# Fused attention and two mixtures of experts: lower parts, one-hots and token numbers moved from VectorE to GpSimd, and another order of VectorE's work

## The chip, the cores and the metric

The kernel runs on one core of a Trainium2 chip. The metric is the device time of one execution in microseconds, the median of several runs. Five engines work side by side, each through its own queue in order: TensorE (PE in the profile; its weight loads are PEld), VectorE (DVE), ScalarE (ACT), GpSimd (POOL) and SyncE (SP). Here SyncE issues the DMAs of the weights and GpSimd the indirect ones, which gather and scatter rows by token number.

## The reference, cut to what matters

Causal attention over 4 batches, 12 heads, 448 positions and 64 channels gives a matrix x of 1792 tokens by 768 channels. Two mixtures of experts follow, each with 8 experts of 768 x 1024 and 1024 x 768.

```
# layer one: only tokens with x @ w_skip > 0 go to an expert
e = argmax(x @ w_gate);  gate = softmax(x @ w_gate)[e]
x = x + gate * (relu(x @ w1[e]) @ w2[e])
# layer two: every token, by the cosine to the experts' embeddings
e = argmax((x/|x|) @ (emb/|emb|).T / tau);  gate = softmax(...)[e]
out = gate * (relu(x @ w1[e]) @ w2[e])
```

## The kernel before, in words

The attention stage comes first and ends at about 230 us. It leaves x in memory, the router's choice for layer one and, for both layers, a table of token numbers by expert in tiles of 128. The expert layers follow: layer one from about 240 to 520 us, a short turn, layer two from 530 us to the end.

**Split numbers.** The products are made in a reduced float32 format. Every operand is therefore split into an upper part (a rounding copy, ScalarE) and a lower part (operand minus upper part, VectorE), and a product takes three terms: upper by upper, lower by upper, upper by lower. For the weights these are split_high (L736) and split_low (L740), on chunks of 128 rows: six chunks of w1, 1024 wide, and eight of w2, 768 wide, per expert. The lower part is written over the raw weights. For the tokens the split is in xt_split (L760, L761), for the activations in split_ht: ScalarE's relu gives the upper part (L772), VectorE the lower one (L773), which reads the transposed h from PSUM and the upper part from SBUF.

**A visit.** One tile of 128 tokens through one expert is a Tile object with two halves, begin and finish. begin has both halves of layer 1 (layer1, L781), the copy of h (copy_h, L940), its transposes (turn_h, L798), its split, and layer 2 over chunks 0 to 5 (layer2, L789). finish has chunks 6 and 7, between them the transposes of the next visit's tokens (L754), and put_y, which scales the result into py. The first visit of an expert also splits its w2 (w2_high, w2_low) between the matmuls, and at the end of begin the first two chunks of the next expert's w1 (ahead, L966 to L970). The last finish of an expert splits chunks 2 to 5 of that w1 and orders the loads of weights further on (L212, L218).

**Branches.** Behind the first begin of an expert stands a branch on the number of further visits (L1107), inside it others (L1088). Where an expert has one visit, every engine steps over the body; an operation behind the branch on a buffer that the body also uses (the three transpose tiles tp among them) waits until the engine it depends on has come out of it. For the input measured here the visits are, by expert 0 to 7: layer one 1, 1, 1, 1, 2, 1, 1, 4; layer two 1, 2, 3, 4, 1, 2, 4, 1; together 30. An expert with two visits uses for its second the tokens of g_r, gathered inside the branch (L1109 in layer two, before finish is written) by a DMA from GpSimd's queue.

**Layer one's router for layer two.** In layer one each visit also finds the expert of layer two for the tokens of the visit before: route_enter (L878: two one-hots multiplied into the table of token numbers), route_turn, route_logits, route_pick with the scatter of py (L856), route_rank, and in finish route_put, which makes row and column (list_place) and from them the one-hots roh and voh (L176, L178). put_y then notes the token numbers: pidx (L812), and in layer one pinv and pv (L814, L815).

**Layer two's norm.** gate_parts gives six steps per visit: the sum of squares (ScalarE, L907), a first guess (L139, L140), three rounds of three small VectorE operations (L143 to L145), and the gate: three operations (L148 to L150), an exponential on ScalarE (L911) and two more (L912, L913). self.step() issues the next of them at the place where it is written, so that its place in begin is its place in the queues. In layer one the list is empty.

The order of everything in this part is written out by hand (manual_schedule): the order of the calls in begin and finish is the order in each engine's queue.

Of the kernel before, what the change touches and what calls it, by code (L numbers as in the profile page):

```python
# [13 lines left out]
ALU = mybir.AluOpType  # L14
# [10 lines left out]
NTOK = B * S  # L25
P = 128
# [4 lines left out]
NONE = 2048  # L31
ROW1 = DM + 1
ROW2 = DM + NE
BIG = float(1 << 20)
# [11 lines left out]
def moe_attention_kernel(tc, qk, vv, w_r, emb, tau, w11, w12, w21, w22, out):  # L46
    nc = tc.nc
# [24 lines left out]
    with ExitStack() as top:  # L72
# [98 lines left out]
        def one_hots(eng, n, row, col, v, roh, voh, which=(0, 1), between=lambda: None):  # L171

            for j in which:
                between()
                if j == 0:
                    eng.tensor_scalar(roh, count[:n], row, None, op0=ALU.is_equal)  # L176
                else:
                    eng.tensor_scalar(voh, count[:n, 0:NCOL], col, v, op0=ALU.is_equal, op1=ALU.mult)  # L178
# [506 lines left out]
        with ExitStack() as ctx:  # L685
# [20 lines left out]
            pidx = keep([P, 1], I32, "pidx")  # L706
# [31 lines left out]
            def split_low(i, c, eng):  # L738
                hi, lo, raw = chunk(i, c)
                eng.tensor_tensor(lo, raw, hi.bitcast(F32), op=ALU.subtract)  # L740
# [61 lines left out]
            def put_y(m, g, idx):  # L802
                for u in range(2):
                    s_ = slice(u * (DM // 2), (u + 1) * (DM // 2))
                    if m == 0:
                        nc.vector.scalar_tensor_tensor(
                            py[:, s_], p2[u], g[:, DM : DM + 1], g[:, s_], op0=ALU.mult, op1=ALU.add)
                    elif u == 0:
                        nc.scalar.activation(py[:, s_], p2[u], AF.Copy, scale=gate2)
                    else:  # L810
                        nc.vector.tensor_scalar(py[:, s_], p2[u], gate2, None, op0=ALU.mult)  # L811
                nc.vector.tensor_copy(pidx, idx)  # L812
                if m == 0:
                    nc.vector.tensor_scalar(pinv, idx, float(NTOK - 1), BIG, op0=ALU.is_gt, op1=ALU.mult)  # L814
                    nc.vector.tensor_scalar(pv, idx, -float(NONE), None, op0=ALU.add)  # L815

            def put_out():
                nc.gpsimd.indirect_dma_start(  # L818
# [23 lines left out]
            def route_pick():  # L842
                mx = rooms["mx2"]
                nc.vector.tensor_reduce(out=mx, in_=pm[:, 0:8], axis=AX.X, op=ALU.max)
                d = py[:, DM:]
                nc.vector.tensor_scalar(d, pm[:, 0:8], mx, None, op0=ALU.subtract)
                eq = rooms["eq2"]
                nc.vector.scalar_tensor_tensor(eq, d, 0.0, wtie[:, 0:8], op0=ALU.is_equal, op1=ALU.mult)
                bm = rooms["bm2"]
                nc.vector.tensor_reduce(out=bm, in_=eq, axis=AX.X, op=ALU.max)  # L850
                nc.vector.tensor_tensor(bm, bm, pinv, op=ALU.max)
                oh = rooms["oh2"]
                nc.vector.tensor_scalar(oh, eq, bm, None, op0=ALU.is_equal)
                nc.vector.tensor_scalar(bm, bm, -float(CT), float(NE * CT), op0=ALU.mult, op1=ALU.add)
                rt.update(base=bm, oh=oh, eq=eq)
                nc.gpsimd.indirect_dma_start(  # L856
                    out=x2, out_offset=bass.IndirectOffsetOnAxis(ap=pidx, axis=0),
                    in_=py, in_offset=None, bounds_check=NTOK - 1, oob_is_err=False)
# [5 lines left out]
            def route_put(fills=None):  # L864
                if fills is None:
                    nc.vector.tensor_tensor(run[:, 1, :], run[:, 1, :], rt["oh"], op=ALU.add)
                rk = rooms["rk2"]
                nc.vector.tensor_tensor_reduce(
                    out=rt["eq"], in0=pm[:, 8:16], in1=rt["oh"], scale=1.0, scalar=0.0,
                    op0=ALU.mult, op1=ALU.add, accum_out=rk)  # L870
                fill = lambda: fills.pop(0)() if fills else None
                row, col = list_place(None, P, rk, rt["base"], None, fill, rooms["lp"])
                roh = rooms["roh2"]
                voh = rooms["voh2"]
                one_hots(nc.vector, P, row, col, pv, roh, voh, between=fill)

            def route_enter(last=False):
                nc.tensor.matmul(pm[:, 16 : 16 + NCOL], rooms["roh2"], rooms["voh2"], start=True, stop=True)  # L878
# [63 lines left out]
            class Tile:  # L942
# [23 lines left out]
                def ahead(self, k):  # L966

                    if self.first and self.i + 1 < len(experts):
                        split_high(self.i + 1, k)
                        split_low(self.i + 1, k, nc.vector)  # L970

                def begin(self):
                    i, route = self.i, self.m == 0 and self.prev
                    if self.m == 1 and self.prev:
                        put_out()
                    self.step()
                    self.w2_high(0, 1, 2, 3)
                    layer1(i, 0, range(4), False)
                    layer1(i, 1, range(3), False)
                    layer1(i, 0, range(4, KC), False)  # L980
                    self.step()
                    layer1(i, 0, range(KC), True)
                    if route:

                        route_enter()
                    self.w2_low(0, 1)
                    copy_h(0)
                    self.w2_high(4)
                    self.step()
                    self.w2_low(2, 3)  # L990
                    self.step()
                    layer1(i, 1, range(3, KC), False)
                    if i == 0 and not self.prev:
                        late_hots()
                        enter_late()
                    if route:
                        route_turn()
                    state["tp"] = 2
                    turned = turn_h(0)
                    self.step()  # L1000
                    split_ht(turned, 0)
                    while self.norm:
                        self.step()
                    layer1(i, 1, range(KC), True)
                    copy_h(1)
                    self.w2_high(5, 6, 7)
                    if route:
                        route_logits()
                    self.w2_low(4)
                    if route:  # L1010
                        route_pick()
                    self.w2_low(5)
                    layer2(i, 0)
                    layer2(i, 1)
                    turned = turn_h(1)
                    split_ht(turned, 4)
                    self.w2_low(6, 7)
                    layer2(i, 2)
                    layer2(i, 3)
                    if route:  # L1020
                        route_rank()
                    self.ahead(0)
                    self.ahead(1)
                    layer2(i, 4)
                    layer2(i, 5)
# [181 lines left out]
```

## Time and profile before

| | us |
|---|---|
| median of 3 runs | 903.12 (901.76 to 904.38) |
| the profiled execution's own time | 902.78 |
| span from its first to its last instruction | 901.1 |
| TensorE busy | 824.0 |
| VectorE busy | 554.4 |
| ScalarE busy | 474.8 |
| GpSimd busy | 135.2 |

The profile is of one execution. In a timeline row stand the start in us from the span's start, the duration, the engine, the line of the kernel and the operation, what is written and read, how many instructions of the kind were merged (xN), and in brackets the engine's idle time before it with what ended it. "DVEq" is VectorE's queue (a branch, a semaphore). A wait for several semaphores is put down to the one that came last, and now and then to the instruction that stands behind the true one.

### The profile page before, as it was taken

How to read it: one execution, taken by the hardware profiler on the slowest of the kernel's cores; microseconds unless marked ns; L12 is line 12 of the kernel's file. 1: busy time of each engine (PE TensorE's matmuls, PEld its weight loads, DVE VectorE, ACT ScalarE, POOL GpSimd, SP SyncE). 2: the span in 40 equal slices, each digit the busy share in tenths (PEclk: the TensorE clock that was granted, in tenths of full speed). 3: DMA queues.
4: the chain of work that ended last, by engine and by line, in shares of the span. 5: the costliest groups of instructions: out<-in, count | busy, mean ns of one | idle time of the engine just before them, and what ended most of it. 6: DMA issues, size and time to landing. Idle time of an engine off the chain costs nothing. (4 is left out here: it accounts for less than half of the span.)

```text
span 901.1 us, 14898 instructions
## 1 busy us (share of the span) xinstructions
PE 824.0 (91%) x4960; PEld 686.5 (76%) x4960; DVE 554.4 (62%) x1641; ACT 474.8 (53%) x1013; POOL 135.2 (15%) x150
## 2 busy tenths in 40 slices
PE   7998989989797899899999879899999998999994
PEld 5665766666487788788899748789889887889884
DVE  5767767776566688378833476665283268574343
ACT  5777666666455466166612336454272256463252
POOL 1132404013201111011010021011111011110100
PEclk9999999999899899999999999999999999999998
DMA  8979565563636487267710354580451086361000
GB/s 243 315 271 299 165 185 165 167 206 139 202 140 258 175 300 286 72 232 300 299 45 28 145 198 159 197 332 21 149 211 51 19 313 267 133 238 41 37 1 18
DMA packets 59032, 158.22 MB, mean 176 GB/s; under 512 B 13013, under 2 KB 23765, under 8 KB 58448
## 3 DMA queue, kind: packets, MB, share of 16 engines
q1 hardware_dynamic: 52816, 139.33, 43.4%
q0 software_dynamic: 6080, 17.29, 5.4%
q8 instruction: 59, 0.97, 0.5%
q14 instruction: 77, 0.63, 0.2%
HBM read 146.45 MB, written 22.92 MB: 188 GB/s over the span
## 5 line engine op out<-in xcount | busy, mean ns | idle before, releaser
L789 PE MATMUL p<-hi,ht 128*128 128x384 f32 x960 | 241.8, 353 | 8.5 <-DVE ht L773 4.6
L740 DVE TENSOR_TENSOR lo<-raw,hi 128x768 fp32r<-128x768 f32 (+1 forms) x218 | 220.6, 1062 | 8.0 <-ACT hi L736 4.5
L781 PE MATMUL p<-hi,xt 128*128 128x512 f32 x720 | 183.3, 403 | 8.0 <-PEq L1088 3.3
L736 ACT CAST hi<-raw 128x768 fp32r<-128x768 f32 (+1 forms) x218 | 187.3, 923 | 0.6 <-DMA raw<-in_w 0.6
L789 PEld LDWEIGHTS p<-hi,ht 128*128 128x128 f32 x960 | 167.8, 191 | 14.7 <-DVE ht L773 10.6
L781 PEld LDWEIGHTS p<-hi,xt 128*128 128x128 f32 x720 | 140.4, 198 | 37.4 <-ACTq L1088 5.1
L321 ACT ACTIVATE pr<-st,mn 112x336 f32<-112x336 f32 x192 | 99.5, 520 | 60.4 <-DVE mn L318 60.4
L789 PE MATMUL p<-lo,ht 128*128 128x384 f32 x480 | 124.3, 340 | 0.4 <-issue 0.4
L773 DVE SCALAR_TENSOR_TENSOR ht<-tp,ht 128x512 fp32r<-128x512 f32 x60 | 41.4, 689 | 115.3 <-ACT ht L772 106.6
L781 PE MATMUL p<-lo,xt 128*128 128x512 f32 x360 | 96.2, 402 | 0.0
L940 ACT COPY hs<-p 128x512 f32<-128x512 f32 x60 | 34.8, 580 | 106.0 <-PE p L781 67.0
L789 PEld LDWEIGHTS p<-lo,ht 128*128 128x128 f32 x480 | 88.7, 191 | 0.5 <-issue 0.5
L760 ACT CAST xt<-tp 128x384 fp32r<-128x384 f32 (+2 forms) x62 | 30.4, 492 | 109.5 <-PE tp L754 108.8
L761 DVE TENSOR_TENSOR xt<-tp,xt 128x384 fp32r<-128x384 f32 (+2 forms) x62 | 33.3, 544 | 84.5 <-ACT xt L760 81.6
L318 DVE CUSTOM_DVE_ANT_0 st<-s,mask 112x336 f32<-112x336 f32 x144 | 63.5, 465 | 29.4 <-PE s L307 17.8
L781 PEld LDWEIGHTS p<-lo,xt 128*128 128x128 f32 x360 | 67.8, 195 | 11.4
L772 ACT ACTIVATE ht<-tp 128x512 fp32r<-128x512 f32 x60 | 36.0, 600 | 55.1 <-PE tp L798 49.4
L331 PE MATMUL tp<-ident,pr 112*112 112x112 f32 x480 | 57.3, 267 | 0.0
L307 PE MATMUL s<-qk 64*112 64x112 f32 (+2 forms) x288 | 49.6, 450 | 7.1 <-DVE mn L318 7.1
L331 PEld LDWEIGHTS tp<-ident,pr 112*112 112x112 f32 x480 | 47.1, 136 | 8.6 <-issue 7.8
L818 POOL DMA_INDIRECT out<-py,pidx x18 | 19.7, 1093 | 207.7 <-ACT hi L736 75.5
L342 PE MATMUL av<-pt,v 112*64 112x448 f32 (+3 forms) x384 | 50.6, 405 | 0.0
(201 smaller groups left out, 908.3 us busy)
## 6 DMA issues: line engine op xcount, KB each, us to landing
raw<-in_w SPq DMA_DIRECT2D x96, 512.0 KB
raw<-in_w SPq DMA_DIRECT2D x128, 384.0 KB
qk<-in_qk SPq DMA_DIRECT2D x23, 896.0 KB
x<-x SPq DMA_DIRECT2D x24, 448.0 KB
v<-in_vv SPq DMA_DIRECT2D x4, 1344.0 KB
qk<-in_qk SPq DMA_DIRECT2D x2, 448.0 KB
g_n<-x,L POOLq DMA_INDIRECT x23, 4.4
out<-py,pidx POOLq DMA_INDIRECT x18, 3.4
```

The costliest lines, as they stand in the source:

```text
L307: nc.tensor.matmul(a[c], src[r : r + 64, c * CP : (c + 1) * CP], src[r : r + 64, S : S + n], start=True, stop=True)
L318: nc.vector.tensor_tensor_reduce(out=so, in0=a[c], in1=mask[:, S - n : S], scale=-0.125, scalar=3.0e38, op0=ALU.add, op1=ALU.min, accum_ou ...
L321: return lambda: nc.scalar.activation(a["pr"][:, OFF[c] * CP : OFF[c] * CP + n], so, AF.Exp, bias=mn, scale=-1.0, accum_out=rs)
L331: nc.tensor.transpose(tp[:, u * CP : (u + 1) * CP], pr[:, o : o + CP], ident[:CP, :CP])
L342: nc.tensor.matmul(av[u * D : (u + 1) * D, j * CP :], v_t[b][:, j, 2 * hp + u, :], pts[2 * g + u][:, o : o + (NCH - j) * CP], start=(j == ...
L736: copy(hi, raw)
L740: eng.tensor_tensor(lo, raw, hi.bitcast(F32), op=ALU.subtract)
L772: nc.scalar.activation(hi, src, AF.Relu)
L773: nc.vector.scalar_tensor_tensor(lo, src, 0.0, hi.bitcast(F32), op0=ALU.max, op1=ALU.subtract)
L781: nc.tensor.matmul(p1[u], xt[:, k, :, j], r[:, u * 512 : (u + 1) * 512], start=(k == 0 and j == 0 and not low), stop=(k == KC - 1 and low))
L789: mm = nc.tensor.matmul(p2[u], l, r[:, u * (DM // 2) : (u + 1) * (DM // 2)], start=(f == 0 and j == 0), stop=(f == FC - 1 and j == len(ter ...
L940: nc.scalar.copy(hs[:, u * 512 : (u + 1) * 512], p1[u])
```

## The change

- ahead: the lower parts of the first two chunks of the next w1 go from VectorE to GpSimd.
- route_put: the one-hots go to GpSimd, but for the call at the turn that has other work to put between (fills).
- put_y: pidx, pinv and pv go to GpSimd.
- begin: the lower part of the first half of h (split_ht) now stands in front of chunks 2 and 3 of w2; of the norm, the first round goes behind chunk 4 of w2, the second between chunks 6 and 7, the third and the gate behind chunk 7.

```
--- before.py
+++ after.py
@@ -809,10 +809,10 @@
                         nc.scalar.activation(py[:, s_], p2[u], AF.Copy, scale=gate2)
                     else:
                         nc.vector.tensor_scalar(py[:, s_], p2[u], gate2, None, op0=ALU.mult)
-                nc.vector.tensor_copy(pidx, idx)
+                nc.gpsimd.tensor_copy(pidx, idx)
                 if m == 0:
-                    nc.vector.tensor_scalar(pinv, idx, float(NTOK - 1), BIG, op0=ALU.is_gt, op1=ALU.mult)
-                    nc.vector.tensor_scalar(pv, idx, -float(NONE), None, op0=ALU.add)
+                    nc.gpsimd.tensor_scalar(pinv, idx, float(NTOK - 1), BIG, op0=ALU.is_gt, op1=ALU.mult)
+                    nc.gpsimd.tensor_scalar(pv, idx, -float(NONE), None, op0=ALU.add)
 
             def put_out():
                 nc.gpsimd.indirect_dma_start(
@@ -872,7 +872,7 @@
                 row, col = list_place(None, P, rk, rt["base"], None, fill, rooms["lp"])
                 roh = rooms["roh2"]
                 voh = rooms["voh2"]
-                one_hots(nc.vector, P, row, col, pv, roh, voh, between=fill)
+                one_hots(nc.vector if fills is not None else nc.gpsimd, P, row, col, pv, roh, voh, between=fill)
 
             def route_enter(last=False):
                 nc.tensor.matmul(pm[:, 16 : 16 + NCOL], rooms["roh2"], rooms["voh2"], start=True, stop=True)
@@ -967,7 +967,7 @@
 
                     if self.first and self.i + 1 < len(experts):
                         split_high(self.i + 1, k)
-                        split_low(self.i + 1, k, nc.vector)
+                        split_low(self.i + 1, k, nc.gpsimd)
 
                 def begin(self):
                     i, route = self.i, self.m == 0 and self.prev
@@ -986,9 +986,6 @@
                     self.w2_low(0, 1)
                     copy_h(0)
                     self.w2_high(4)
-                    self.step()
-                    self.w2_low(2, 3)
-                    self.step()
                     layer1(i, 1, range(3, KC), False)
                     if i == 0 and not self.prev:
                         late_hots()
@@ -997,10 +994,8 @@
                         route_turn()
                     state["tp"] = 2
                     turned = turn_h(0)
-                    self.step()
                     split_ht(turned, 0)
-                    while self.norm:
-                        self.step()
+                    self.w2_low(2, 3)
                     layer1(i, 1, range(KC), True)
                     copy_h(1)
                     self.w2_high(5, 6, 7)
@@ -1009,12 +1004,17 @@
                     self.w2_low(4)
                     if route:
                         route_pick()
+                    self.step()
                     self.w2_low(5)
                     layer2(i, 0)
                     layer2(i, 1)
                     turned = turn_h(1)
                     split_ht(turned, 4)
-                    self.w2_low(6, 7)
+                    self.w2_low(6)
+                    self.step()
+                    self.w2_low(7)
+                    while self.norm:
+                        self.step()
                     layer2(i, 2)
                     layer2(i, 3)
                     if route:
```

## Rows read from the trace of the kernel before

**Rows 1.** The page's first part: busy time and share of the span by engine.

```profile
PE 824.0 (91%) x4960; PEld 686.5 (76%) x4960; DVE 554.4 (62%) x1641; ACT 474.8 (53%) x1013; POOL 135.2 (15%) x150
```

**Rows 2.** Waits of TensorE from 240 to 901 us: total, times, longest.

```profile
PE tp L754 <- DVEq L1107: 9.5, 6, 2.7
...
PE p L789 <- DVE ht L773: 4.6, 4, 1.7
...
PE p L789 <- DVE tn_a L148: 3.8, 3, 1.3
...
PE p L781 <- DVEq L1088: 2.5, 2, 1.5
...
PE pm L878 <- DVE voh L178: 1.4, 6, 0.5
```

**Rows 3.** Timeline of VectorE, expert 5 of layer one: start, us, instruction.

```profile
404.15 4.09 DVE L740 TENSOR_TENSOR lo<-raw,hi 128x768 fp32r<-128x768 f32 x4
...
416.57 0.25 DVE L176 TENSOR_SCALAR roh<-count,lq_r 128x128 f16<-128x128 bf16 x1
...
416.74 0.30 DVE L178 TENSOR_SCALAR voh<-count,lq_o,pv 128x112 f16<-128x112 bf16 x1
```

**Rows 4.** Timeline of TensorE: the first transposes behind four branches; idle time in brackets.

```profile
287.26 0.52 PE L754 MATMUL tp<-ident,g_r 128*128 128x128 f32 x3 [2.74 <-DVEq L1107]
...
408.40 0.52 PE L754 MATMUL tp<-ident,g_r 128*128 128x128 f32 x3 [1.24 <-DVEq L1107]
...
552.85 0.52 PE L754 MATMUL tp<-ident,g_r 128*128 128x128 f32 x3 [0.39 <-PEq L1107]
...
751.18 0.55 PE L754 MATMUL tp<-ident,g_r 128*128 128x128 f32 x3 [2.40 <-DVEq L1107]
```

**Rows 5.** Timeline of VectorE, first visit of expert 1 of layer two.

```profile
563.42 1.83 DVE L740 TENSOR_TENSOR lo<-raw,hi 128x768 fp32r<-128x768 f32 x2
...
566.21 0.69 DVE L773 SCALAR_TENSOR_TENSOR ht<-tp,ht 128x512 fp32r<-128x512 f32 x1
```

**Rows 6.** Timeline of ScalarE: expert 0 of layer two, then expert 1.

```profile
548.77 1.99 ACT L736 CAST hi<-raw 128x1024 fp32r<-128x1024 f32 x2
...
563.62 0.60 ACT L772 ACTIVATE ht<-tp 128x512 fp32r<-128x512 f32 x1
...
570.89 1.99 ACT L736 CAST hi<-raw 128x1024 fp32r<-128x1024 f32 x2
...
573.88 0.51 ACT L760 CAST xt<-tp 128x384 fp32r<-128x384 f32 x1 [1.00 <-PE tp L754]
...
583.71 0.59 ACT L940 COPY hs<-p 128x512 f32<-128x512 f32 x1 [5.39 <-PE p L781]
```

**Rows 7.** Timeline of TensorE, expert 1 of layer two.

```profile
566.95 0.97 PE L789 MATMUL p<-hi,ht 128*128 128x384 f32 x4 [1.25 <-DVE tn_a L148]
...
577.09 1.23 PE L781 MATMUL p<-hi,xt 128*128 128x512 f32 x4 [0.87 <-PEq L1088]
```

**Rows 8.** Groups of instructions by line: busy us, mean ns, idle us before.

```profile
L568 POOL TENSOR_TENSOR lo<-raw,hi 128x1024 fp32r<-128x1024 f32 x6 | 14.2, 2363 | 65.0 <-ACT hi L637 65.0
...
L176 POOL TENSOR_SCALAR roh<-count,lp_r 112x128 f16<-112x128 bf16 x25 | 14.9, 597 | 118.9 <-DVE lp_o L168 96.6 <-PE idle L129 22.3
...
L178 POOL TENSOR_SCALAR voh<-count,lp_o,ids 112x112 f16<-112x112 bf16 x24 | 17.7, 739 | 0.0
```

**Rows 9.** Windows view: busy us (count) of PE, PEld, DVE, ACT, POOL; clock, DMA, GB/s.

```profile
288.00:292.00 4.00, 4.00 (x16) 3.82 (x15) 2.24 (x4) 3.50 (x5) 0.00 (x0) 0.57 1.00 374
```

**Rows 10.** DMA view: gathers, their count and median us from issue to landing.

```profile
g_n<-x,L POOLq DMA_INDIRECT x23, 4.4
...
g_r<-x,ir POOLq DMA_INDIRECT x7, 6.6
```

**Rows 11.** L359's duration, min/median/max ns, and a row of GpSimd's timeline.

```profile
L359 DVE TENSOR_SCALAR rs<-rs x24: 157/160/596, 21.3 to 225.4; 112x8 f32<-112x8 f32 x24
...
148.41 0.60 POOL L176 TENSOR_SCALAR roh<-count,lp_r 112x128 f16<-112x128 bf16 x1
```

More of the change, by code (lines that the diff above doesn't have):

```diff
@@ L811, in put_y @@
                         nc.vector.tensor_scalar(py[:, s_], p2[u], gate2, None, op0=ALU.mult)
-                nc.vector.tensor_copy(pidx, idx)
+                nc.gpsimd.tensor_copy(pidx, idx)
                 if m == 0:
-                    nc.vector.tensor_scalar(pinv, idx, float(NTOK - 1), BIG, op0=ALU.is_gt, op1=ALU.mult)
-                    nc.vector.tensor_scalar(pv, idx, -float(NONE), None, op0=ALU.add)
+                    nc.gpsimd.tensor_scalar(pinv, idx, float(NTOK - 1), BIG, op0=ALU.is_gt, op1=ALU.mult)
+                    nc.gpsimd.tensor_scalar(pv, idx, -float(NONE), None, op0=ALU.add)
             def put_out():
@@ L874, in route_put @@
                 voh = rooms["voh2"]
-                one_hots(nc.vector, P, row, col, pv, roh, voh, between=fill)
+                one_hots(nc.vector if fills is not None else nc.gpsimd, P, row, col, pv, roh, voh, between=fill)
             def route_enter(last=False):
@@ L969, in ahead @@
                         split_high(self.i + 1, k)
-                        split_low(self.i + 1, k, nc.vector)
+                        split_low(self.i + 1, k, nc.gpsimd)
                 def begin(self):
@@ L988, in begin @@
                     self.w2_high(4)
-                    self.step()
-                    self.w2_low(2, 3)
-                    self.step()
                     layer1(i, 1, range(3, KC), False)
@@ L999, in begin @@
                     turned = turn_h(0)
-                    self.step()
                     split_ht(turned, 0)
-                    while self.norm:
-                        self.step()
+                    self.w2_low(2, 3)
                     layer1(i, 1, range(KC), True)
@@ L1011, in begin @@
                         route_pick()
+                    self.step()
                     self.w2_low(5)
@@ L1016, in begin @@
                     split_ht(turned, 4)
-                    self.w2_low(6, 7)
+                    self.w2_low(6)
+                    self.step()
+                    self.w2_low(7)
+                    while self.norm:
+                        self.step()
                     layer2(i, 2)
```

## The prediction

> **What bounds the kernel now.** I read the page first: TensorE is busy for 824.0 of 901.1 us [rows 1], so only its idle moments can be won, and a microsecond taken from another engine counts only where TensorE waits for it. So the second view is TensorE's own waits in the two expert layers, 240 to 901 us [rows 2]. The reader should see three kinds that this change touches. First, six waits of 9.5 us in all of the transposes (L754) for VectorE to come out of the branch on a second visit (L1107). Second, seven waits for the activations' lower part, 4.6 us under the name of L773 and 3.8 us under that of a norm step which stands right behind it (8.4 us in all). Third, six short waits of L878 for VectorE's one-hots, 1.4 us in all. Two waits (2.5 us) at L1088 are for VectorE too.
>
> The third view is the timeline around such waits. In expert 5 of layer one VectorE comes out of its lower part of h at 404.15 and makes four lower parts in 4.09 us, two of w2 and two of the next w1 [rows 3]; TensorE, ready at 407.16, may transpose only at 408.40 [rows 4]. In expert 1 of layer one the same wait is 2.74 us, in expert 4 of layer two 2.40 us; where VectorE is early, the branch alone takes 0.39 us [rows 4]. Subtracting from the 9.5 us, three waits are of 1.24 us and one of 0.69 us. In layer two the order on VectorE shows: two parts of w2 at 563.42, norm steps, and only at 566.21 the lower part of h, whose upper part (563.62, 0.60 us) had been there since 564.22 [rows 5, 6]; TensorE loses 1.25 us [rows 7].
>
> **Lower parts of w1 to GpSimd.** Two 768-wide parts take 1.83 us [rows 5], the run of four 4.09 us, so VectorE is spared 2.26 us before every branch. GpSimd takes 2363 ns for one such part in the attention stage [rows 8], so 4.7 us for two, beginning when ScalarE has made the upper part. They are read by TensorE some 8 us after the branch, so their length alone costs nothing there; what is queued behind them on GpSimd does (below). How a GpSimd subtract and a VectorE subtract get along is in no row. From below the hold is 0; from above one GpSimd part, 2.36 us, in front of w2's last lower part. I take 0, since VectorE starts its four parts closer together than each takes (its next one is always there already), and keep 2.36 for the first rival. Without a hold VectorE leaves the branch before TensorE gets there in experts 1, 2, 3, 5 and 6 of layer one: **expert 1 gains 2.3** (2.74 less 0.39), experts 3, 5, 6 gain 0.85 each and expert 2 0.3.
>
> The clock hangs on expert 1: after its wait the granted clock is 0.57 on the mean of 288 to 292 us, so 1.2 GHz for most of it, with TensorE busy for all 4.00 us [rows 9]. That is 1.7 us of its work (0.43 of 4 us). With the idle time in front of it gone I take back **1.2 us**, the larger part, since TensorE is paced by ScalarE's upper parts for some of that stretch; between 0 and 1.7.
>
> **One-hots and token numbers.** On GpSimd the two one-hots take 597 and 739 ns, on VectorE the second ends 0.47 us after the first began [rows 3, 8]. So they end 0.85 us later, and I add 0.1 us for passing from one engine to another: 0.95 us. L878 already waited for them [rows 2], at five visits of layer one and at the turn between the layers, and nothing stands between. In experts 3, 5 and 6 the 0.95 is put against the 0.85 won at the branch: **+0.1 each**, and in expert 2, where the one-hots had slack, 0.3 against 0.3, again about +0.1. In expert 4 and 7, whose first visit has no such wait, +0.95 stands against 0.6 less at L1088, where VectorE is spared its one-hots (0.47 us) and three 0.06 us steps: **+0.75 together**. At the turn VectorE reaches py earlier, so 0.65 remains. On the three or four later visits of expert 4 and 7 VectorE had idle time of several us: nothing. The copies of pidx, pinv and pv go behind the one-hots in GpSimd's queue and delay the next gathers by under 1 us, which are wanted over 8 us later: nothing; without that cover the cost is that 1 us once per expert.
> Layer one: -2.3 -1.2 +0.4 +0.75 +0.65 = **-1.7 us**.
>
> **The order in layer two.** With two parts of w2 and two norm rounds moved behind it, the lower part of h is ready at 564.9, before TensorE wants it at 565.7: the 1.25 us go. What is late next is the norm. Its exponential sits in ScalarE's queue, now in front of the upper parts of the next w1 (570.89, 1.99 us) and of xt (573.88) [rows 6]. In the first visit of expert 1, VectorE after 568.8 has the lower part of h (0.61), two of w2 (0.87 each), two rounds (0.5 each) and the finish (0.6): the exponential starts at 572.8 and takes 0.5 us, then come 1.9 us of upper parts, and xt at 575.2 instead of 573.88. TensorE could begin the next visit at 577.09 - 1.25 = 575.84 and gets its xt at about 576.2 [rows 7]: 0.9 of 1.25 us are kept. The other visits, by the same steps with their own times:
> - experts 2, 3 and 6: waits of 1.65, 1.25 and 1.29, less 0.3 each: -1.3, -1.0, -1.0. Expert 7 has no next w1: -1.25.
> - expert 4: 1.25 won, but ScalarE now comes out of the branch last, 750.7 against 751.18 for the transposes [rows 4]: -0.4.
> - expert 0 has no w2 to hide in: ScalarE's upper parts at 548.77 start 2.9 us later [rows 6], its last ends at 553.75, and the transposes, at 552.85 before [rows 4], go to 553.85: +1.0.
> - experts 1 and 5 have exactly two visits, and **the gather of g_r for the second is queued on GpSimd behind the two lower parts**. In expert 1 these run from 574.4 to 579.1; a gather takes 4.4 us to land in the median of 23 (6.6 for these seven, which fell among weight loads) [rows 10], so 583.4. The sum of squares (1.0 us) stands in front of ScalarE's copy of h, which goes from 583.71 [rows 6] to 584.5; with the 0.9 won this is **+0.5**. In expert 5, where only 0.4 us was to be won, the copy goes 2.3 us later by the same steps, of which I count **+1.85** for TensorE. With 6.6 us each is 2.2 more.
> Layer two: +1.0 +0.5 -1.3 -1.0 -0.4 +1.85 -1.0 -1.25 = **-1.6 us**.
>
> **Sum:** -3.3 us. The profiled execution took 902.78 us (span 901.1), 0.34 below the median of 903.12, so **899.8 us** against that median. A measurement of this kernel can tell about 0.3% (2.7 us) from no change.
>
> **Rivals.**
> 1. *GpSimd holds VectorE up (slower).* A GpSimd operation that reads SBUF does hold a VectorE operation in one place: L359, 160 ns in the median, once took 596 ns beside the one-hot of 148.41, until that one's end [rows 11]. That was a tensor_scalar on 8 columns; against it, where L359 met only the tail of GpSimd's long subtracts it kept its usual time, so it is no hold of every kind. If the subtracts exclude each other and GpSimd gets in between w2's last two parts, VectorE comes out of the branch at about the time of before or later: expert 1 wins nothing and keeps its clock (3.6 us against the forecast), experts 3, 5, 6 lose 1.2 each and expert 2 0.9. That is 8.1 us: **907.9**. It decides as soon as GpSimd's part starts ahead of w2's last one; in layer two the exponential keeps them apart. The Trainium skill says so in "SBUF — State Buffer", Who interferes with whom: a VectorE instruction with two SBUF inputs contends with a GpSimd instruction that reads SBUF, and the second one blocks until the first is through. By that rule the sum would be 907.9 if GpSimd comes first, 899.8 if VectorE does; no run here shows it for two subtracts.
> 2. *The late norm costs nothing.* If the gathers land early and ScalarE has slack, expert 0 gives 0, expert 1 -0.9 and expert 5 -0.4: 4.65 us less, **895.2**. For it: before, ScalarE idled 5.39 us in front of that copy of h in expert 1 [rows 6].
> 3. *Nothing moves.* VectorE is relieved, but TensorE still finds the branch closed in expert 1, since ScalarE or the semaphores behind L1107 are as late, and the clock falls as before: 3.5 us more, **903.3**. For it: L1107's wait names VectorE's queue, not an operation [rows 2].
>
> **How the numbers follow.** Forecast 0.40 (its own range 897.8 to 902), first rival 0.32, second 0.13, third 0.15. I hold the first rival below the forecast because it needs two things, the exclusion and GpSimd's getting in first. Under 900.4 lie two thirds of the forecast and the second rival: 0.40 faster. The third rival, a third of the forecast and a little of the first are the same: 0.30. Slower: 0.30. The range 896.0 to 908.5 leaves out half of the second rival and a third of the first.
>
> **What would show it.** Right: no wait on L773 over 0.4 us in layer two; L754 in layer one waits 0.4 us; L878 waits 1.0 us for GpSimd; the exponential stands in front of ScalarE's upper parts of w1, and experts 1 and 5 of layer two show ScalarE waiting for g_r. Wrong: VectorE's subtracts of w2 beside GpSimd's take over 2 us, or GpSimd's take well over 2.36; or the transposes wait for GpSimd.

## The result: slower by 1.3%, and the profile after

The changed kernel takes **913.84 us** in the median of 4 runs (912.49 to 918.94), beside 903.15 for the kernel before on the same chip: ratio 1.0131, 95% interval 1.0106 to 1.0156. 899.8 was forecast, 896.0 to 908.5 as the range, so both sign and range missed. The profiled execution took 913.95 us (span 912.2).

The busy times on the page of the changed kernel; [rows 1] holds those of before:

```profile
PE 827.9 (91%) x4960; PEld 689.4 (76%) x4960; DVE 532.4 (58%) x1535; ACT 475.0 (52%) x1013; POOL 248.9 (27%) x256
```

From its groups by line, shapes kept apart (busy us, mean ns, idle before), the subtracts of both engines:

```profile
L740 DVE TENSOR_TENSOR lo<-raw,hi 128x768 fp32r<-128x768 f32 x128 | 134.9, 1093 | 5.6 <-ACT hi L736 2.8 <-DMA raw<-in_w 1.7 <-issue 1.1
L740 POOL TENSOR_TENSOR lo<-raw,hi 128x1024 fp32r<-128x1024 f32 x30 | 79.1, 2654 | 107.2 <-ACT hi L736 107.1
```

VectorE was relieved of 22 us of work, though its 128 parts of w2 take 17.9 us longer than the 117.0 (953 ns each) of before, and TensorE still ends later. Its own waits in the expert layers, 240 to 915 us, against [rows 2]:

```profile
PE tp L754 <- DVEq L1107: 11.4, 6, 2.4
PE pm L878 <- POOL voh L178: 9.3, 7, 1.6
PE p L789 <- DVE ht L773: 5.3, 1, 5.3
PE p L781 <- ACTq L1088: 5.1, 4, 2.0
...
PE p L781 <- ACT xt L760: 3.0, 3, 1.0
```

The 8.4 us of waits for the activations' lower part in layer two are gone, as forecast. But the branch waits (9.5 us before) are longer instead of shorter, L878 has gone from 1.4 to 9.3 us, layer one has a new wait of 5.3 us, and ScalarE holds up the next visit.

**Two subtracts at once.** VectorE, GpSimd and TensorE around expert 3 of layer one (timelines; start, duration, engine, line, what, xN, idle before):

```profile
336.78 4.01 DVE L740 TENSOR_TENSOR lo<-raw,hi 128x768 fp32r<-128x768 f32 x2
...
336.86 6.18 POOL L740 TENSOR_TENSOR lo<-raw,hi 128x1024 fp32r<-128x1024 f32 x2 [0.85 <-ACT hi L736]
...
340.95 0.52 PE L754 MATMUL tp<-ident,g_r 128*128 128x128 f32 x3 [1.47 <-DVEq L1107]
```

Two parts of w2 take VectorE 1.8 us where it is alone; here it takes 4.01, the four parts of before 4.09 [rows 3]. GpSimd needs 6.18 us for two parts whose like took 2363 ns each [rows 8]: each engine waits out the other's instruction. So TensorE's wait of 1.24 us [rows 4] became 1.47, where 0.4 was forecast. In expert 2 VectorE lost twice in a row:

```profile
306.33 5.82 DVE L740 TENSOR_TENSOR lo<-raw,hi 128x768 fp32r<-128x768 f32 x1 [0.33 <-ACT hi L736]
...
306.67 4.65 POOL L740 TENSOR_TENSOR lo<-raw,hi 128x1024 fp32r<-128x1024 f32 x2
...
312.80 1.65 PE L789 MATMUL p<-hi,ht 128*128 128x384 f32 x4 [5.35 <-DVE ht L773]
```

One part of w2 took 5.82 us beside GpSimd's two, the lower part of h stood behind it, and TensorE waited 5.35 us. The window 312 to 316 us of TensorE (length, busy, granted clock, DMA share, GB/s; the clock's upper level, 2.4 GHz, is 1.00) shows the clock after it:

```profile
312.00:316.00 4.00, 2.93 (x8) 0.50 0.02 4
```

0.50, that is 1.2 GHz, for a TensorE that had stood still. In expert 1 the branch wait is 2.32 us, hardly less than the 2.74 of before [rows 4], but behind it the clock stays at 1.00, where it had been at 0.57 on the mean of the window behind that wait [rows 9]. The first transposes and the window 286 to 290 us (columns as in [rows 9]):

```profile
285.94 0.52 PE L754 MATMUL tp<-ident,g_r 128*128 128x128 f32 x3 [2.32 <-DVEq L1107]
...
286.00:290.00 4.00, 4.00 (x24) 3.77 (x25) 2.09 (x3) 3.46 (x5) 2.03 (x1) 1.00 0.78 292
```

**One-hots.** In expert 2 again, GpSimd and TensorE:

```profile
294.36 0.62 POOL L176 TENSOR_SCALAR roh<-count,lq_r 128x128 f16<-128x128 bf16 x1 [6.33 <-PE p L781]
294.98 0.75 POOL L178 TENSOR_SCALAR voh<-count,lq_o,pv 128x112 f16<-128x112 bf16 x1
...
295.78 0.21 PE L878 MATMUL pm<-voh,roh 128*128 128x112 f16 x1 [1.28 <-POOL voh L178]
```

**The late norm.** ScalarE and TensorE at the end of the first visit of expert 2 in layer two, then VectorE and TensorE at that of expert 0:

```profile
619.09 0.60 ACT L772 ACTIVATE ht<-tp 128x512 fp32r<-128x512 f32 x1
624.14 0.30 ACT L911 ACTIVATE ex<-g_r,tn_a 128x8 f32<-128x8 f32 x1 [4.46 <-DVE tn_a L150]
...
624.44 1.98 ACT L736 CAST hi<-raw 128x1024 fp32r<-128x1024 f32 x2
626.33 0.88 ACT L760 CAST xt<-tp 128x384 fp32r<-128x384 f32 x2
...
626.87 1.33 PE L781 MATMUL p<-hi,xt 128*128 128x512 f32 x3 [1.04 <-ACT xt L760]
...
556.68 0.16 DVE L913 RECIPROCAL gate<-gs 128x1 f32<-128x1 f32 x1
...
559.65 0.55 PE L754 MATMUL tp<-ident,g_r 128*128 128x128 f32 x3 [2.38 <-DVEq L1107]
```

ScalarE stands idle for 4.46 us in front of the exponential, then makes the upper parts of w1 and only then xt, for which TensorE waits 1.04 us; before, it waited 1.66 us in the middle of this visit. In expert 0 the wait at the branch has grown from 0.39 [rows 4] to 2.38 us. It is a wait for VectorE's queue, though VectorE had finished the gate at 556.84 us, 2.8 us before the transposes; what keeps its queue until then the profile doesn't show. The clock behind it is at 0.75 on the mean of the window 559 to 563 us (length, busy times of TensorE, its weight loads, VectorE, ScalarE and GpSimd, clock, DMA share, GB/s):

```profile
559.00:563.00 4.00, 3.35 (x16) 3.27 (x17) 0.94 (x2) 2.36 (x4) 3.17 (x2) 0.75 1.00 364
```

At the end of the first visit of expert 5 TensorE waits for ScalarE at L1088, and the clock falls behind that wait. The gather of g_r comes late, as forecast, but the copy of h behind it still has to wait for TensorE (TensorE, ScalarE, and the window 786 to 790 us):

```profile
785.96 0.57 PE L781 MATMUL p<-hi,xt 128*128 128x512 f32 x1 [1.96 <-ACTq L1088]
...
792.42 0.85 ACT L907 ACTIVATE yt<-g_r 128x768 f32<-128x768 f32 x1 [6.55 <-DMA g_r<-x,ir]
...
793.76 0.59 ACT L940 COPY hs<-p 128x512 f32<-128x512 f32 x1 [0.40 <-PE p L781]
...
786.00:790.00 4.00, 3.84 (x9) 2.82 (x10) 0.58 (x2) 0.00 (x0) 3.67 (x4) 0.57 0.03 8
```

### The profile page after: what moved, and what is told of

Read it like the earlier page. It is cut to its first block, busy times and chain, and to the rows that moved or that the text cites. A ratio compares the mean times of both kernels' runs of the same rounds, so it can differ in the third digit from the quotient of the medians.

```text
span 912.2 us, 15027 instructions
## 1 busy us (share of the span) xinstructions
PE 827.9 (91%) x4960; PEld 689.4 (76%) x4960; DVE 532.4 (58%) x1535; ACT 475.0 (52%) x1013; POOL 248.9 (27%) x256
## 5 line engine op out<-in xcount | busy, mean ns | idle before, releaser
L740 DVE TENSOR_TENSOR lo<-raw,hi 128x768 fp32r<-128x768 f32 (+1 forms) x188 | 204.6, 1135 | 5.9 <-ACT hi L736 3.0
L781 PE MATMUL p<-hi,xt 128*128 128x512 f32 x720 | 187.6, 409 | 15.0 <-ACTq L1088 5.1
L781 PEld LDWEIGHTS p<-hi,xt 128*128 128x128 f32 x720 | 142.6, 201 | 50.3 <-issue 8.9
L773 DVE SCALAR_TENSOR_TENSOR ht<-tp,ht 128x512 fp32r<-128x512 f32 x60 | 41.4, 690 | 142.7 <-ACT ht L772 142.7
L740 POOL TENSOR_TENSOR lo<-raw,hi 128x1024 fp32r<-128x1024 f32 x30 | 79.1, 2654 | 107.2 <-ACT hi L736 107.1
## 6 DMA issues: line engine op xcount, KB each, us to landing
qk<-in_qk SPq DMA_DIRECT2D x23, 896.0 KB
```

The lines of the kernel that those rows point to most:

```text
L773: nc.vector.scalar_tensor_tensor(lo, src, 0.0, hi.bitcast(F32), op0=ALU.max, op1=ALU.subtract)
L781: nc.tensor.matmul(p1[u], xt[:, k, :, j], r[:, u * 512 : (u + 1) * 512], start=(k == 0 and j == 0 and not low), stop=(k == KC - 1 and low))
```

## The experiments

All times are medians; "before" was run with each of them and lay between 902.5 and 903.2.

### The change less one part

**Without the lower parts on GpSimd (e1).**

```
-                        split_low(self.i + 1, k, nc.gpsimd)
+                        split_low(self.i + 1, k, nc.vector)
```

> The change without the lower parts of the next w1 on GpSimd (they go back to VectorE; one-hots, token numbers and the order stay as changed). The changed kernel takes 913.8 us, the kernel before 903.1. Hold theory (GpSimd's and VectorE's subtracts of two SBUF inputs shut each other out): VectorE's lower parts of w2 on second visits go back from 3.1 to about 0.95 us, the wait of 5.3 us at L789 for L773 in expert 1 goes, with it some 1.5 us of half clock, and the gathers are no longer queued behind the subtracts: about 906 us (905 to 908). Rival, one-hots (the seven waits of L878, 9.3 us, are the loss): at most 3 us better than the changed kernel, 911 or more.

925.58 us, 1.0267 (1.0239 to 1.0295): 12 us worse than the change, which neither theory had. Layer one came out 3.5 us better than in the changed kernel; the loss is in layer two. TensorE and VectorE of this kernel, expert 0:

```profile
553.93 2.36 DVE L740 TENSOR_TENSOR lo<-raw,hi 128x1024 fp32r<-128x1024 f32 x2 [0.59 <-ACT hi L736]
...
560.87 0.90 PE L754 MATMUL tp<-ident,g_r 128*128 128x128 f32 x3 [7.10 <-DVEq L1107]
```

With the norm late, VectorE waits for the exponential and then for the upper parts before it may start on w1. So with the norm late the two parts of w1 cost less on GpSimd: this visit is 3.2 us longer than before in the changed kernel and 8.2 here. What holds VectorE from the end of its parts at 556.3 to its next operation at 562.39 isn't in the profile, which shows nothing of it between its branch and 560.80. (The Trainium skill, "Runtime: NRT & Kernel Launch", Instruction fetch mechanics, says that a taken branch to a page not at hand stalls its engine until that is fetched. That would fit: the trace has one load of instructions in this gap, but doesn't tell for which engine, so no run here shows it.)

**Without the one-hots on GpSimd (e2).**

```
-one_hots(nc.vector if fills is not None else nc.gpsimd, P, row, col, pv, roh, voh, between=fill)
+one_hots(nc.vector, P, row, col, pv, roh, voh, between=fill)
```

> The change without the one-hots on GpSimd (they go back to VectorE; token numbers, lower parts and the order stay as changed). Hold theory: only the waits of L878 go, from 9.3 us to about 1.6, while VectorE has 0.47 us more in front of the branch at four visits: about 908 us (906 to 910). One-hot theory: 904 or less, since hardly anything else costs. Rival, the waits of L878 are covered by what comes behind them: 912 or more.

903.75 us, 1.0013 (0.9993 to 1.0033): the one-hot theory's number. The waits of L878 are back at 1.4 us, but the part of 5.82 us is gone too (3.16 in its place): of the 10 us that this run is below the changed kernel, 6.8 fall in that one visit. So it can't say that the hold costs nothing.

**With the norm early (e3).** The steps stand as in e4 below, the rest as in the change.

> The change with the norm steps early again: all rounds ahead of the turn of h and the exponential right behind the lower part of h, w2's parts 2 and 3 behind them; one-hots, token numbers and lower parts on GpSimd stay. Late-norm theory (the exponential in front of ScalarE's upper parts costs layer two its gain): layer two loses its 6.4 us over before and wins some of the 8.4 us of L773's waits as well: 904 to 907. Hold theory without a late norm: GpSimd's parts now start earlier in layer two and meet VectorE's, the 0.3 to 0.5 us that a first visit won are replaced by holds: 911 to 915.

927.29 us, 1.0284 (1.0259 to 1.0308): worse than either theory. VectorE, GpSimd and TensorE in the first visit of expert 1, layer two:

```profile
576.67 6.08 DVE L740 TENSOR_TENSOR lo<-raw,hi 128x768 fp32r<-128x768 f32 x2
...
576.50 5.43 POOL L740 TENSOR_TENSOR lo<-raw,hi 128x1024 fp32r<-128x1024 f32 x2 [7.33 <-ACT hi L736]
...
579.75 0.62 PE L789 MATMUL p<-lo,ht 128*128 128x384 f32 x2 [0.60 <-DVE lo L740]
...
582.80 0.61 PE L789 MATMUL p<-lo,ht 128*128 128x384 f32 x2 [1.40 <-DVE lo L740]
...
586.38 0.77 PE L781 MATMUL p<-hi,xt 128*128 128x512 f32 x1 [2.61 <-PEq L1088]
```

With the exponential early ScalarE has w1's upper parts ready early, GpSimd's parts meet both of VectorE's, and TensorE waits for w2's lower parts themselves. It then reaches its own branch (L1088) so late that 2.61 us of it stay uncovered. The late norm keeps the two engines apart in layer two.

### One part alone on the kernel before

**The order alone, norm early (e4).** In begin, nothing else:

```
                     self.w2_high(4)
                     self.step()
-                    self.w2_low(2, 3)
                     self.step()
...
                     split_ht(turned, 0)
                     while self.norm:
                         self.step()
+                    self.w2_low(2, 3)
```

> The kernel before with the order alone: w2's parts 2 and 3 behind the lower part of h, the norm steps all ahead of them (two rounds in front of the turn of h, finish and exponential right behind its lower part); nothing goes to GpSimd. If only the late norm eats what the order wins: six or seven first visits of layer two lose their waits of 1.25 us for L773, 903.1 - 7 = 896 us (895 to 898). Rival (something else is as late as the lower part of h, xt or the copy of h by ScalarE): 900 or more. Layer one unchanged, since VectorE's parts have slack there.

**893.83 us**, 0.9910 (0.9890 to 0.9930): faster than both kernels, and the fastest here that leaves nothing out. TensorE's first waits in layer two, 540 us to the end; [rows 2] had 8.4 us for the third of them:

```profile
PE tp L754 <- DVEq L1107: 2.4, 1, 2.4
PE p L781 <- PEq L1088: 2.4, 2, 1.2
PE p L789 <- DVE ht L773: 2.3, 7, 0.3
```

**The lower parts alone on GpSimd (e5), the one-hots alone (e6), the whole new order alone on VectorE (e7).** e7 is begin of the changed kernel, as in the diff, with nothing on GpSimd.

```
-                        split_low(self.i + 1, k, nc.vector)
+                        split_low(self.i + 1, k, nc.gpsimd)
...
-one_hots(nc.vector, P, row, col, pv, roh, voh, between=fill)
+one_hots(nc.vector if fills is not None else nc.gpsimd, P, row, col, pv, roh, voh, between=fill)
```

The first pair of lines is e5, the second e6.

> The kernel before with the two lower parts of the next w1 alone on GpSimd (order, one-hots and token numbers as before). Hold theory: GpSimd's and VectorE's parts take turns, some 3.1 us each where they meet, and with the exponential early ScalarE has the upper parts ready early, so they meet in layer two as well: 912 us or more (up to 920). Forecast's theory (no hold worth counting, VectorE earlier at the branch): 899 to 901. If the hold exists but stays off TensorE's path: 902 to 906.

> The kernel before with the one-hots alone on GpSimd (token numbers stay on VectorE). One-hot theory: L878 waits some 1.2 us at seven places instead of 1.4 us in all, and nothing behind it takes that up: 902.5 + 8 to 10 = 910 to 913 us. Forecast's theory (0.95 us more at each, half of it given back by a VectorE that is spared them): 905 to 907. If the waits only take the place of others: 903.

> The kernel before with the whole new order of the change (w2's parts 2 and 3 behind the lower part of h, norm late) and nothing on GpSimd. Late-norm theory: the norm's wait for ScalarE now stands on VectorE in front of the lower parts of the next w1, so VectorE is late at the branch and ScalarE's upper parts are late too: 912 to 918 us, some 20 more than with the norm early (893.8). Forecast's theory (0.3 us lost at each first visit): 897 to 900.

e5: 909.14 us, 1.0087 (1.0055 to 1.0119), between the hold theory's 912 and the 902 to 906 of a hold off TensorE's path; the forecast's 899 to 901 is out. By visits, counted as in the table further down, layer one of e5 is 6.4 us shorter than before, though its branch waits there add up to 7.0 us, hardly less than before, and layer two is 9.2 us longer, 8.3 of them in experts 1 and 5. There TensorE waits 2.5 us at L1088 and runs at about half clock behind that (0.50 and 0.62 on the means of 574 to 578 and 778 to 782 us). e6: 909.34 us, 1.0091 (1.0057 to 1.0124), its interval too wide to part 907 from 910, but the waits are those of the changed kernel, to the tenth:

```profile
PE pm L878 <- POOL voh L178: 9.3, 7, 1.6
```

e7: 923.18 us, 1.0210 (1.0158 to 1.0261), its four runs between 916.1 and 927.0, some 29 us more than e4 where the late-norm theory had 20. 9.0 us of it are one wait at L754 for VectorE's branch in expert 4, of the kind seen in e1.

### What GpSimd reads

In e8 and e14 the two parts of before are replaced on GpSimd, by writes alone and by an operation with one input; e9 is the changed kernel with the writes of e8. In all three the lower part of two chunks of each next w1 is left out. The first three added lines are those of e8 and e9, the others those of e14.

```
-                        split_low(self.i + 1, k, nc.vector)
+                        lo = chunk(self.i + 1, k)[1]
+                        for n in (DF, DF, DF // 2):
+                            nc.gpsimd.memset(lo[:, :n].bitcast(F32), 0.0)
...
+                        lo, raw = chunk(self.i + 1, k)[1:]
+                        nc.gpsimd.tensor_scalar(lo, raw, 0.0, None, op0=ALU.mult)
```

> The kernel before with GpSimd only writing in the place of the two lower parts of the next w1: three memsets per part (1024, 1024 and 512 wide, some 2.4 us), so GpSimd reads nothing; the lower part of the first two chunks of each next w1 is left out of the computation. If the hold is between reads of the two engines: VectorE's parts of w2 stay at 0.95 us and the time is 899 to 905 us. If any work of GpSimd on SBUF holds VectorE: parts of 3 us again and the time of the kernel that really subtracts there.

> The kernel before with GpSimd reading one operand instead of two in the place of the two lower parts (it multiplies the raw part by zero, so the lower part of the first two chunks of each next w1 is left out). If one read is enough for the hold: VectorE's parts of w2 that meet it take well over 0.95 us, up to GpSimd's own duration more, and TensorE's waits behind the branch stay near 9 us. If only two reads hold: 0.95 us as with writes alone and 893 us.

The same two parts of w2 in expert 1 of layer one (timelines; VectorE, then GpSimd) in e5 (two inputs), e14 (one) and e8 (none):

```profile
283.71 3.98 DVE L740 TENSOR_TENSOR lo<-raw,hi 128x768 fp32r<-128x768 f32 x2
...
284.09 5.86 POOL L740 TENSOR_TENSOR lo<-raw,hi 128x1024 fp32r<-128x1024 f32 x2 [5.78 <-ACT hi L736]
```
```profile
284.63 2.65 DVE L740 TENSOR_TENSOR lo<-raw,hi 128x768 fp32r<-128x768 f32 x2
...
285.01 5.95 POOL L971 TENSOR_SCALAR lo<-raw 128x1024 fp32r<-128x1024 f32 x2 [6.28 <-ACT hi L736]
```
```profile
283.98 1.82 DVE L740 TENSOR_TENSOR lo<-raw,hi 128x768 fp32r<-128x768 f32 x2
...
284.33 5.04 POOL L972 MEMSET lo<- 128x1024 f32 x6 [6.03 <-ACT hi L736]
```

GpSimd is as busy at the same place in all three, some 5 to 6 us, and VectorE's pair takes 3.98, 2.65 and 1.82 us. Writes hold nothing up, one input does by 0.8 us, two by 2.2. e8 takes 893.23 us, 0.9895 (0.9860 to 0.9930), e14 895.72, 0.9921 (0.9898 to 0.9943). One input does hold VectorE, but the rest of that expectation (waits near 9 us) fell: the hold left the pair shorter than the four parts of before. TensorE's waits of e8 at the branch (L1109 there, L1107 before) show it open: 0.4 us a time, which is what the forecast had counted on.

```profile
PE tp L754 <- PEq L1109: 2.9, 7, 0.5
...
PE tp L754 <- DVEq L1109: 0.6, 1, 0.6
```

> The whole change, but GpSimd only writes where it made the two lower parts of the next w1 (three memsets per part, some 2.5 us; the lower part of the first two chunks of each next w1 is left out of the computation). Hold theory: the wait of 5.35 us for L773 in expert 2, the branch waits of experts 1, 3, 5 and 6 of layer one (2.3 and three of 1.45 instead of 0.4) and the half clock behind them go: 10 to 12 us less than the changed kernel's 913.8, 902 to 904; what then remains above 893 (writing only, nothing else changed) is the one-hots. Rival (in the changed kernel the late norm keeps the subtracts apart, so the hold is not its loss): 910 or more.

906.39 us, 1.0048 (1.0029 to 1.0066): 7.4 us less than the changed kernel, where 10 to 12 were expected. The wait of 5.35 us is gone, and the branch waits of layer one are at 0.4 us. TensorE's waits:

```profile
PE pm L878 <- POOL voh L178: 9.3, 7, 1.6
PE p L781 <- ACTq L1090: 5.0, 4, 2.0
PE tp L754 <- DVEq L1109: 4.7, 2, 2.4
...
PE p L781 <- ACT xt L760: 3.0, 3, 1.0
```

What is left beside the one-hots is the late norm: ScalarE's late xt, and the branch waits of 2.4 us in experts 0 and 4 of layer two, the first of them new [rows 4], for a VectorE that waits for the exponential before it can come to the branch. In expert 4 the gate ends 0.5 us before the transposes; in expert 0 it ends 2.8 us before, as in the changed kernel, so the exponential alone doesn't account for that wait.

### The norm's place without the hold

e13 is e9 with the norm's steps where e4 has them; the steps at the late places are gone:

```
                     self.w2_high(4)
+                    self.step()
+                    self.step()
...
                     turned = turn_h(0)
+                    self.step()
                     split_ht(turned, 0)
+                    while self.norm:
+                        self.step()
                     self.w2_low(2, 3)
```

> The whole change with GpSimd only writing where it made the two lower parts (906.4 us with the norm late), and the norm steps early: two rounds ahead of the turn of h, the exponential right behind its lower part, w2's parts 2 and 3 behind it; the lower part of the first two chunks of each next w1 is left out. If the late norm costs by itself (the exponential in front of ScalarE's upper parts): the 2.0, 2.0 and 1.9 us lost in experts 0, 1 and 5 of layer two go and some 1.0 more is won at each of the other first visits, 896 us (894 to 899). Rival (the late place costs only by the hold that it was to avoid): 905 or more.

896.45 us, 0.9927 (0.9908 to 0.9945), as the late-norm theory had it. The losses in experts 0 and 5 are gone. That in expert 1 is not: its first visit is 2.7 us longer than before in e13 too, so the late norm is at most a part of what costs there. TensorE waits 1.11 us at its own branch (L1090 here, L1088 before), and 2.61 us behind it for nothing that the profile names. At the branch on further visits (L1109 here, L1107 before) TensorE doesn't wait for VectorE any more, not in expert 4 either, where before had 2.40 us [rows 4]; its first waits in e13, behind those for the one-hots (9.3 us as in e9):

```profile
PE p L781 <- PEq L1090: 3.9, 5, 1.1
PE tp L754 <- PEq L1109: 3.4, 8, 0.5
```

### Further versions

Built on e4, all on VectorE. e10 moves route_put in finish; e11, beyond that, leaves ahead the lower part of chunk 0 only and has low(1, 2); e12 leaves ahead none and has low(0, 1, 2).

```
+                    if route:
+                        route_put()
                     low(2)
                     high(3)
...
-                    if route:
-                        route_put()
                     put_y(self.m, self.g, idx)
```

> The best order so far (w2's parts 2 and 3 behind the lower part of h, norm early, all on VectorE, 893.8 us) with the ranks and one-hots of the router issued on VectorE ahead of the lower parts 2 to 5 of the next w1 instead of behind them. If the seven waits of L878 (1.4 us) go and nothing takes their place: 892 to 893. Rival (the lower parts, 0.6 us later, are missed by TensorE in the next visit): 894 to 897.

> As the one with the one-hots earlier, and the lower part of chunk 1 of the next w1 made behind the branch, in the last visit's tail, instead of ahead of it. VectorE comes 0.95 to 1.2 us earlier to the branch: the three waits of 1.24 us and the one of 2.5 us at L754 shrink to about 0.4 and 1.3, some 4 us: 888 to 890. Rival (VectorE is late with the next visit's lower parts): 893 or more.

> As the former, with the lower parts of chunks 0 and 1 both behind the branch. If VectorE's load ahead of the branch alone sets the branch: all waits of L754 at 0.4 us, 886 to 889. Rival (six lower parts, 7.3 us, stand in the tail and the first is wanted by TensorE some 5 us into the next visit): 893 or more, with waits of L781 for L740.

895.89 us, 0.9924 (0.9893 to 0.9954); 906.54, 1.0046 (1.0026 to 1.0066); 925.31, 1.0253 (1.0227 to 1.0280). e10 can't be told from e4; in the other two the rival held. In e12 the branch waits did shrink, and TensorE paid more in the next visit (lower-part products of layer 1):

```profile
L781 PE MATMUL p<-lo,xt 128*128 128x512 f32 x360 | 108.5, 419 | 21.3 <-DVE lo L740 17.5 <-DMA raw<-in_w 3.8
```

## Why the prediction was wrong

Four kernels in a chain, each with something more, give the loss in medians: before 902.5; lower parts off VectorE with no reads on GpSimd (e8) 893.2; with the one-hots, the token numbers and the order of e4 (e13) 896.5; with the norm late (e9) 906.4; with GpSimd's reads (the change) 913.8. That is -9.3, +3.2, +9.9 and +7.4. The visits below are read from one profiled execution of each kernel, and for those four steps these executions give -8.2, -2.7, +13.4 and +8.8: the first, third and fourth have the same sign, the second isn't clear.

- **Lower parts to GpSimd, without a hold: right.** The forecast's gains in layer one (2.3, 1.2 for the clock, 2.85 at experts 2, 3, 5 and 6) come to 6.4 us. By visits e8 gains 3.2 in expert 1, 1.8 in expert 2 and 0.8 to 0.9 each in experts 3, 5 and 6, with branch waits of 0.4 (0.6 in expert 1). It also gains 3.2 us in expert 4 of layer two, whose branch wait of 2.40 us [rows 4] goes as well, which the forecast didn't count.
- **The hold taken as 0: the first step that failed.** It costs 7.4 us in the changed kernel, where VectorE's second part of w2 takes 3.1 us beside GpSimd's. The reason given, that VectorE's parts start closer together than each takes, speaks of VectorE alone and says nothing of two engines. The first rival had the mechanism, and for experts 3, 5 and 6 also place and price: 1.2 us each, and by visits the changed kernel loses 1.1, 1.0 and 1.1 against e9. It had also that in layer two the late exponential keeps the engines apart: in the changed kernel only one of VectorE's operations is held there. That its sum of 8.1 us comes near the 7.4 is luck. Expert 1, which it priced at 3.6, is 1.2 us shorter than in e9: the clock didn't fall behind its branch wait, and a later wait (L840), 3.04 us in e9, is 0.39. Expert 2, priced at 0.9, is 5.5 us longer, by the one part of 5.82 us. The forecast gave this rival a chance of 0.32. There was also more to go by than its one row: L359 took 546 ns a second time, at 93.05 us in before, beside another one-hot of GpSimd. By the rule named there, of the Trainium skill, "SBUF — State Buffer", Who interferes with whom, the sum would be 907.9, since GpSimd got in first; the trace agrees with the rule on reads and writes (3.98 us for the pair with reads, 1.82 with writes alone). It doesn't agree that the second always blocks until the first is through: beside a GpSimd operation with one input, of 3.2 us, VectorE's part was held for 0.8 us only.
- **One-hots and token numbers: price nearly right, cover wrong.** 0.95 us each was forecast, 1.1 measured (9.3 less 1.4 us, over seven). But in four experts it was to be paid from the time won at the branch, and the hold had taken that: the first visits of experts 3, 5 and 6 in layer one lost 1.33, 1.35 and 1.33 us, not 0.1 each. Without the hold, in e9, they lost 0.2, 0.4 and 0.3. The token numbers were not tried alone.
- **The order in layer two: the second step that failed.** From the start of each visit's second-layer products to the next visit's, after less before, layer two gives:

| first visit of expert | forecast | measured |
|---|---|---|
| 0 | +1.0 | +3.2 |
| 1 | +0.5 | +2.7 |
| 2 | -1.3 | -0.5 |
| 3 | -1.0 | -0.1 |
| 4 | -0.4 | -0.95 |
| 5 | +1.85 | +2.05 |
| 6 | -1.0 | -0.1 |
| 7 | -1.25 | -0.7 |

With 0.7 us in a later visit of expert 2 (a wait of 1.34 us at L1088) these are the 6.4 us that layer two lost. The waits of L773 went and the exponential came late, as described. What was wrong is what stands behind it. For experts 2, 3 and 6 "less 0.3 each" was carried over from expert 1, whose next visit begins behind a branch wait (0.87 us of its own before the change) that hides most of ScalarE's lateness; without it the wait for xt is 1.0 us, and 0.1 to 0.5 of each gain is left. In expert 0 only ScalarE was followed out of the branch: VectorE's queue comes out of it later still, 2.8 us behind the gate, so the wait grew by 2.0 us instead of 1.0, and behind it the clock fell again. In experts 1 and 5 the path was wrong. The gather landed late, and ScalarE waited 6.6 us for it in both, but its copy of h then still waited for TensorE (2.53 and 0.40 us): the gather cost nothing. TensorE waited for ScalarE earlier, at the branch L1088 (1.96 us in each, where before it waited 0.87 and 0.89 for its own queue), and the clock fell behind that (0.54 on the mean of 588 to 592 us in expert 1, 0.57 in expert 5). That expert 5's +2.05 lies near the forecast's +1.85 is luck.
- **The rivals of no cost and of nothing moved** are out: by e9 against e13 the late norm costs 9.9 us, though expert 1 is no shorter without it, and e8 shows the branch opening.

What stays open: why in expert 2 of layer one GpSimd got both its parts in ahead of a part of VectorE that had started 0.34 us earlier by the profile, where elsewhere they took turns; it was seen in the changed kernel alone, and by visits it is 5.5 of the 8.8 us that GpSimd's reads cost there. And what VectorE does behind the branch in e1 and e7, and in expert 0 of the changed kernel. And what ends TensorE's wait behind L1088 in expert 1 of layer two, 1.30 us in the changed kernel and 2.61 in e13. And the +3.2 of the chain's second step is more than the one-hots (+6.8) and the order (-8.7) sum to when each is alone, while the -2.7 of the profiled executions is less; the runs don't say whether one of them changes beside a VectorE without the lower parts, and the interval of the one-hots' run is wide.

## What to carry to other kernels

A subtract of two SBUF operands moved from VectorE to GpSimd isn't off VectorE while VectorE has such subtracts of its own: here, where the two overlapped, each waited out the other, so count GpSimd's duration as VectorE's, or keep them apart in time. A step that is postponed takes its waits with it: look up what stands behind it on every engine that it touches, not only what it frees, and don't carry a hidden lateness over to a place without the cover. And changes made together should be priced apart: here one reordering alone was worth 9 us, hidden in a change that lost 11.

## What the runs showed of the hardware

- GpSimd's reads hold VectorE by degrees: of the pairs above the second part is the one held, and with the first at 0.86 us (0.95 less what the two overlap) it took 0.96 us beside writes, 1.79 beside an operation with one input and 3.12 beside one with two. GpSimd is held as well: 3.1 us a part in expert 3 (6.18 for two), 2.36 where it is alone. VectorE's lower part of h, which reads one operand from PSUM, kept its 0.7 us throughout.
- What a branch costs an engine depends on how much work its queue has ahead of it. TensorE's branch L1088 took 3.40 us of its queue in expert 1 of layer two, before and in e3 alike (the median of its 18 times is 0.19). Before, its queue came to it 2.70 us ahead of the end of its products, and TensorE stood idle for 0.87 us [rows 7]; in e3, where it had been stopped by w2's lower parts just ahead of the branch, 0.96 us ahead of it, and the idle time was 2.61. Why the branch takes 3.40 us isn't shown.
